# Attention with 192 queries and 1,024 keys: GpSimd issues 121 of 128 partitions of each group's store

## The chip, the cores and the metric

The kernel runs on one core of one Trainium2 chip. The core has five engines that run side by side and meet only at semaphores: TensorE (matrix products, PE in the profile), VectorE (DVE), ScalarE (ACT), GpSimd (POOL) and SyncE (SP, which here only issues transfers). Data moves between the main memory (HBM) and the on-chip memory (SBUF) on 16 DMA engines, which all queues share. A transfer is issued by an instruction on SyncE, ScalarE or GpSimd, and each of these has a queue of its own. TensorE writes its products to a second on-chip memory, PSUM.

The metric is the time of one execution on the device in microseconds (us), as the median of several runs.

## The reference

The reference is softmax attention over 16 x 32 = 512 heads. Each has 192 queries, 1,024 keys and 1,024 values of 128 numbers, all bfloat16:

```python
B, H, Sq, Sk, D = 16, 32, 192, 1024, 128
scale = q.shape[-1] ** -0.5
scores = jnp.einsum("bhqd,bhkd->bhqk", q, k) * scale
p = softmax(scores, axis=-1)
return jnp.einsum("bhqk,bhkd->bhqd", p, v)
```

Keys and values are 134 MB each, queries and output 25 MB each.

## The kernel before

**Groups, pairs and units.** The 512 heads are worked in 32 groups of 16 (`G=16`). A group has 8 pairs of heads (`PPG`). The 2 x 192 query rows of a pair make three units of 128 rows: unit A (128 rows of the first head), unit B (128 of the second) and unit S (64 of each). So a group has 24 units (`UPG`), and a unit is a tile of 128 query rows by 1,024 keys. Two pairs, six units in the order A0 B0 A1 B1 S0 S1, make one *period*; a group has four periods. Unit numbers in the text are those inside a group: unit 12 is A0 of the third period, unit 14 its A1, unit 18 is A0 of the fourth period, and unit 21 its B1.

**One unit.** TensorE makes the scores into PSUM (`s_ps`, "qk"). VectorE scales them into `ss` and finds the row's extreme in the same instruction (line 333). Four of six units then go to ScalarE, which takes the exponential into `x_sb` (line 374). The other two (A0 and B1, "shifted") go to GpSimd, which subtracts the extreme (line 208), and ScalarE takes the exponential later. TensorE transposes `x_sb` in 8 blocks ("tr", into `pt_ps`), ScalarE copies the result to `pt_sb` ("ev", lines 383 and 385), TensorE multiplies it with the values ("pv", into `o_ps`), and VectorE divides by the row sums into `ob` (line 358).

**Order.** The order of each engine is written out by hand in `PE_ORDER`, `DVE_ORDER` and `ACT_ORDER`; a tick in these lists means the same unit of the period before. GpSimd runs the shifts in the order of units and nothing else. Every engine runs its list in order, and a wait stops all that stands behind it on that engine. TensorE's transpose of a shifted unit waits for its shift; the transpose of B1 comes in the period after its scores.

**Buffers and transfers.** Keys (`kt`), queries (`qt`) and values (`vs`) of a group have two buffers each, as has the output `ob`. Keys and queries are transposed by the DMA itself (lines 148 and 152). The first two groups are loaded at the start. From then on:

- SyncE, for each group g, waits until TensorE has made all scores of group g (`s_qk`), since its buffer is used again. It then issues the keys and queries of group g + 2, and then waits for the output of group g and stores it. The store is cut by partitions into three transfers, 0 to 79, 80 to 123 and 124 to 127. The last group's output is stored in four pieces of 128 partitions each.
- ScalarE issues the values of the next group after the copy of unit 12 (`VALUES_AFTER`). Before that it waits until the same group's keys have landed (`sxk`, line 393).
- VectorE, before the first output of a group, waits until the store from that half of `ob`, two groups back, has landed (`sst`, line 354).

One row of the output has 128 numbers, 256 bytes. A partition holds 24 such rows of a group, which lie apart in main memory.

## Time and profile before

| What | Before |
|---|---|
| median of 3 runs | 1189.44 us (1187.03 to 1191.16) |
| the profiled execution | 1188.88 us, its span 1187.1 us |
| mean granted TensorE clock | 0.993 |
| TensorE busy | 1125.9 us (95%) |
| VectorE busy | 1087.6 us (92%) |
| ScalarE busy | 1080.6 us (91%) |
| GpSimd busy | 485.8 us (41%) |
| moved by DMA | 321.26 MB, mean 271 GB/s |
| packets | 790,348, of them 724,641 under 512 B |
| SyncE's queue (q1) | 192.95 MB |
| ScalarE's queue (q10) | 125.83 MB |

The profile was taken in one execution, so its parts are compared with 1188.88 us and not with the median. The span is the time from the first to the last instruction of the program. Busy times of the engines overlap and don't add up to the span. In the lists of the profile a name such as "ob<-o_ps" means that a tile is written from another; "L208" is a line of the kernel; "x256" is a count. SPq and ACTq are the transfer-issuing instructions of SyncE and ScalarE; their duration is that of the issue and not that of the transfer. The DMA share is the summed time of packets over 16 engines, and since packets overlap within an engine it can exceed 1.

### The profile page before, as it was taken

Reading aid. Unit: us, or ns where it says so; the run is one execution under the profiler, and the core shown is the slowest. Engines: PE = TensorE matmul, PEld = TensorE weight load, DVE = VectorE, ACT = ScalarE, POOL = GpSimd, SP = SyncE. Lnnn points to the kernel's source line nnn. Section 1 sums busy time; section 2 is a strip of 40 time slices with the busy share of each in tenths; the row PEclk is TensorE's granted clock in tenths of the full one; section 3 lists DMA queues with packets and bytes.
Section 4 is the critical chain, followed back from the end, with each engine's and each line's share of the span. In section 5 each row is a group of like instructions: output and inputs, shape, how many; then the busy total and the mean of one; then the engine's idle time right before and its main releaser. Section 6 shows DMA issues by size and latency. Waiting matters only on the chain.

```text
span 1187.1 us, 38884 instructions
## 1 busy us (share of the span) xinstructions
PE 1125.9 (95%) x18432; PEld 845.9 (71%) x15360; DVE 1087.6 (92%) x2304; ACT 1080.6 (91%) x1793; POOL 485.8 (41%) x262
## 2 busy tenths in 40 slices
PE   5699999999999999999999999999999999999998
PEld 2477776777777776777777767777777776677776
DVE  5589998999999998999999989999999999899997
ACT  4679998999999998999999988999999998899998
POOL 2234443444444434443444434344444343444442
PEclk9899999999999999999999999999999999999999
DMA  9999999999999999999999999999999999999981
GB/s 231 249 280 303 289 285 254 260 299 293 287 293 248 256 290 288 280 283 258 279 298 284 284 265 242 290 296 282 288 266 267 295 284 290 259 267 277 297 246 40
DMA packets 790348, 321.26 MB, mean 271 GB/s; under 512 B 724641, under 2 KB 724641, under 8 KB 790177
## 3 DMA queue, kind: packets, MB, share of 16 engines
q1 hardware_dynamic: 728257, 192.95, 84.0%
q10 hardware_dynamic: 61920, 125.83, 28.7%
q8 instruction: 132, 2.16, 0.7%
q14 instruction: 39, 0.32, 0.1%
HBM read 134.22 MB, written 25.17 MB: 134 GB/s over the span
## 4 chain that ended last, share of the span: by engine, by line
PE 43%; DMA 39%; ACT 11%; SPq 5%; ACTq 1%; issue 0%; DVE 0%
DMA kt<-in_k_dram 39%; PE o_ps L221 15%; PE pt_ps L221 15%; PE s_ps L221 14%; ACT x_sb L374 6%; SPq L148 4%; ACT pt_sb L385 3%; ACT pt_sb L383 2%; ACTq L138 1%; SPq L152 1%; SPq L138 0%; DMA vs<-in_v_dram 0%; DVE ob L358 0%; ACTq L393 0%; DVE rinv L356 0%
## 5 line engine op out<-in xcount | busy, mean ns | idle before, releaser
L333 DVE TENSOR_SCALAR_CACHE_REDUCE ss<-s_ps 128x1024 f32<-128x1024 f32 x768 | 919.5, 1220 | 83.2 <-PE s_ps L221 69.7
L208 POOL TENSOR_TENSOR x_sb<-ss,nb 128x1024 bf16<-128x1024 f32 x256 | 485.1, 1895 | 689.3 <-DVE ss L333 574.1
L374 ACT ACTIVATE x_sb<-ss,nb 128x1024 bf16<-128x1024 f32 x512 | 584.9, 1144 | 13.0 <-DVE ss L333 13.0
L306 PEld LDWEIGHTS <-pt_sb 128*128 128x128 bf16 (+1 forms) x8192 | 440.9, 104 | 194.9 <-issue 101.7
L221 PE MATMUL o_ps<-vs,pt_sb 128*128 128x128 bf16 (+1 forms) x8192 | 494.9, 219 | 0.4 <-DMA vs<-in_v_dram 0.3
L221 PE MATMUL s_ps<-kt,qt 128*128 128x512 bf16 (+1 forms) x2048 | 465.2, 385 | 24.2 <-DMA qt<-in_q_dram 23.7
L221 PE MATMUL pt_ps<-ident,x_sb 128*128 128x128 bf16 x6144 | 449.9, 220 | 33.4 <-ACT pt_sb L383 15.9
L280 PEld LDWEIGHTS <-x_sb 128*128 128x128 bf16 x6144 | 368.9, 98 | 101.5 <-issue 100.7
L385 ACT ACTIVATE pt_sb<-pt_ps 128x512 f32<-128x512 f32 x512 | 306.3, 598 | 84.6 <-PE pt_ps L221 51.5
L383 ACT ACTIVATE pt_sb<-pt_ps 128x1024 bf16<-128x1024 bf16 x256 | 260.3, 1017 | 3.6 <-PE pt_ps L221 3.6
L221 PE MATMUL o_ps<-ones,pt_sb 128*128 128x1 bf16 x2048 | 189.3, 165 | 0.0
L358 DVE TENSOR_TENSOR ob<-o_ps,rinv 128x384 bf16<-128x384 f32 x256 | 142.6, 557 | 8.7
L264 PEld LDWEIGHTS <-qt 128*128 128x128 bf16 (+1 forms) x1024 | 79.3, 103 | 41.6 <-DMA qt<-in_q_dram 18.7
L374 ACT ACTIVATION_READ_ACCUMULATOR x_sb<-ss,nb 128x1 f32 x512 | 100.3, 196 | 0.0
L333 DVE DVE_READ_ACCUMULATOR ss<-s_ps 128x1 f32 x768 | 63.7, 83 | 0.0
L356 DVE RECIPROCAL rinv<-o_ps 128x1 f32<-128x1 f32 x256 | 41.8, 163 | 4.3 <-PE o_ps L221 4.3
L346 DVE RECIPROCAL rinv<-rs 128x2 f32<-128x2 f32 x256 | 41.0, 160 | 1.1 <-ACT x_sb L374 1.1
L374 ACT ACT_TABLE_LOAD x1 | 1.3, 1283 | 0.8 <-PEq L418 0.8
L200 POOL TENSOR_SCALAR_AFFINE_SELECT ident<-ones 128x128 bf16<-128x128 bf16 x1 | 0.3, 294 | 0.1
L198 POOL MEMSET ones<- 128x128 bf16 x1 | 0.2, 205 | 0.3 <-POOLq L418 0.3
L418 POOL MEMSET const-float32-0.0<- 128x1 f32 x1 | 0.1, 99 | 0.3 <-issue 0.3
L418 POOL MEMSET const-bfloat16-1.0<- 128x1 bf16 x1 | 0.1, 102 | 0.0
(2 smaller groups left out, 0.2 us busy)
## 6 DMA issues: line engine op xcount, KB each, us to landing
vs<-in_v_dram ACTq DMA_DIRECT2D x30, 4096.0 KB, 16.3
out_dram<-ob SPq DMA_DIRECT2D x31, 480.0 KB
out_dram<-ob SPq DMA_DIRECT2D x31, 264.0 KB
vs<-in_v_dram SPq DMA_DIRECT2D x1, 4096.0 KB, 15.1
vs<-in_v_dram SPq DMA_DIRECT2D x1, 2048.0 KB, 10.4
vs<-in_v_dram SPq DMA_DIRECT2D x1, 1536.0 KB, 8.9
out_dram<-ob SPq DMA_DIRECT2D x31, 24.0 KB
kt<-in_k_dram SPq DMA_TRANSPOSE x34, 21.1
```

The source lines that it names most:

```text
L148: e.dma_start_transpose(kt[:, s, :, a * 128:b * 128], kf[h0 + a:h0 + b].rearrange("g (p t) d -> (g p) (t d)", t=KT_TILES),).then_inc(sems[ ...
L208: gp.tensor_tensor(x_sb[:, u % NX, :], ss[:, u % NSS, :], nb[:, u % NSS: u % NSS + 1].to_broadcast([128, SK]), ALU.subtract,).then_inc(s_x ...
L221: return pe.add_instruction(mybir.InstMatmult(name=nc.get_next_instruction_name(), engine=mybir.EngineType.PE, ins=[pe.lower_ap(x), pe.low ...
L264: pe.ldweights(w, tile_position=at)
L280: pe.ldweights(w, is_transpose=True, tile_position=(0, 0))
L306: pe.ldweights(w, tile_position=at)
L333: dve.tensor_scalar(ss[:, u % NSS, :], s_ps[u % 2][:].rearrange("p t k -> p (t k)"), -scale, None, ALU.mult, ALU.min, accum_out=nb[:, u % ...
L356: dve.reciprocal(rinv[:, pr % 2, sel], o_ps[pr % 2][:, 3, sel]).then_inc(s_ri, 1)
L358: dve.tensor_tensor(ob[:, so, pg], o_ps[pr % 2][:, 0:3, :], rinv[:, pr % 2, 0:3].unsqueeze(2).to_broadcast([128, 3, 128]), ALU.mult,).then ...
L374: act.activation(x_sb[:, u % NX, :], ss[:, u % NSS, :], ACT_FN.Exp, bias=nb[:, u % NSS: u % NSS + 1], scale=-1.0, accum_out=rs[:, pr % NRS ...
L383: act.activation(pt_sb[:, u % NPT], pt_ps[u % 2][:], ACT_FN.Exp, scale=-1.0).then_inc(s_ev, 1)
L385: act.activation(words(pt_sb[:, u % NPT]), words(pt_ps[u % 2][:]), ACT_FN.Copy).then_inc(s_ev, 1)
```

## The change

The store of each group but the last is split in two. GpSimd issues partitions 0 to 120 as one transfer, SyncE the other 7. GpSimd does this in the group after, in its list behind the shift of unit 18, once ScalarE has made the copy of unit 14 (`POOL_STORE=(18, 14)`) and VectorE all outputs of the group stored. SyncE issues its 7 partitions where it issued the three transfers. GpSimd's stores have semaphores of their own (`ssp`); VectorE waits for both before it writes to that half of `ob` again, and SyncE waits for both at the end. The stores of the last group are as before.

```diff
-  STORE_PARTS=((0, 80), (80, 124), (124, 128)), VALUES_AFTER=("ev", 12)):
+  POOL_STORE=(18, 14), POOL_PARTS=121, VALUES_AFTER=("ev", 12)):
...
+        ssp = [sem("ssp%d" % i) for i in range(NSO)]
...
         def store_cnt(g):
-            return 16 * len(STORE_PARTS) * (g // NSO + 1)
+            return 16 * (g // NSO + 1)
...
+        def store(e, g, a, b, lo, hi, sm):
+            rows = of[g * G + 2 * a:g * G + 2 * b].rearrange("h r d -> (h r) d").rearrange("(n p) d -> p n d", p=128)
+            e.dma_start(
+                rows[lo:hi],
+                ob[lo:hi, g % NSO, a:b].rearrange("p pg y d -> p (pg y) d"),
+            ).then_inc(sm[g % NSO], 16)
...
             def stores(g, a, b):
-                so = g % NSO
                 e.wait_ge(s_on, g * PPG + b)
-                rows = ...
-                for lo, hi in (((0, 128),) if g == NGR - 1 else STORE_PARTS):
-                    e.dma_start(rows[lo:hi], ob[lo:hi, so, a:b]...).then_inc(sst[so], 16)
+                store(e, g, a, b, 0 if g == NGR - 1 else POOL_PARTS, 128, sst)
...
             for so in range(min(NSO, NGR)):
-                n = len(range(so, NGR - 1, NSO)) * len(STORE_PARTS)
+                n = len(range(so, NGR - 1, NSO))
...
                 e.wait_ge(sst[so], 16 * n)
+                e.wait_ge(ssp[so], 16 * len(range(so, NGR - 1, NSO)))
...
+            unit, copy = POOL_STORE
             for u in range(NU):
                 if shifted(u):
                     shift(u)
+                g = u // UPG - 1
+                if u % UPG == unit and g >= 0:
+                    gp.wait_ge(s_ev, u - unit + copy + 1)
+                    gp.wait_ge(s_on, (g + 1) * PPG)
+                    store(gp, g, 0, PPG, 0, POOL_PARTS, ssp)
...
                 if pg == 0 and g >= NSO:
                     dve.wait_ge(sst[so], store_cnt(g - NSO))
+                    dve.wait_ge(ssp[so], store_cnt(g - NSO))
```

More of the change, by code (lines that the diff above doesn't have):

```diff
@@ L34, in _attention_kernel @@
 def _attention_kernel(nc, q, k, v, out, G=16, NS=2, NSS=5, NX=4, NPT=5,
-                      FIRST=((0, 2), (2, 8), (8, 16)), LAST=((0, 4), (4, 6), (6, 7), (7, 8)), STORE_PARTS=((0, 80), (80, 124), (124, 128)), VALUES_AFTER=("ev", 12)):
+                      FIRST=((0, 2), (2, 8), (8, 16)), LAST=((0, 4), (4, 6), (6, 7), (7, 8)), POOL_STORE=(18, 14), POOL_PARTS=121, VALUES_AFTER=("ev", 12)):
     B, H, SQ, D = q.shape
@@ L166, in stores @@
             def stores(g, a, b):
-                so = g % NSO
                 e.wait_ge(s_on, g * PPG + b)
-                rows = of[g * G + 2 * a:g * G + 2 * b].rearrange("h r d -> (h r) d").rearrange(
-                    "(n p) d -> p n d", p=128)
-                for lo, hi in (((0, 128),) if g == NGR - 1 else STORE_PARTS):
-                    e.dma_start(
-                        rows[lo:hi],
-                        ob[lo:hi, so, a:b].rearrange("p pg y d -> p (pg y) d"),
-                    ).then_inc(sst[so], 16)
+                store(e, g, a, b, 0 if g == NGR - 1 else POOL_PARTS, 128, sst)
             n = len(FIRST)
```

## The prediction

> **What bounds the kernel now.** I read the engine totals first, then SyncE's queue, ScalarE around its load of the values, the chain of waits, the DMA rates by stage, and last the gap on GpSimd that the new instruction goes into.

> ```profile
> PE 1125.9 (95%) x18432; PEld 845.9 (71%) x15360; DVE 1087.6 (92%) x2304; ACT 1080.6 (91%) x1793; POOL 485.8 (41%) x262
> ```

> Three engines are over 90% busy, so little is left between them; what is left has to be found by stage. The loop over 31 groups repeats, so one group's cycle is the unit to measure. ScalarE issues one load of values per group, and these are the first and last of them (30 issues, 29 cycles), from the instructions of line 138:

> ```profile
> L138 ACTq DMA_DIRECT2D vs<-in_v_dram x30: 374/375/432, 90.1 to 1133.5; - x30
> ```

> (1133.5 - 90.1) / 29 = 35.98 us a group. What would the engines alone take? In the chain of waits, TensorE's double transposes (x16) mark the four periods of a group. Here are two periods that nothing outside delayed, the second of them holding ScalarE's load issue:

> ```profile
> 259.27 1.00 PE pt_ps L221 x16
> ...
> 267.90 1.00 PE pt_ps L221 x16
> ...
> 276.79 1.00 PE pt_ps L221 x16
> ```

> 8.63 and 8.89 us (8.64 where it is read elsewhere): an undelayed group is 3 x 8.64 + 8.89 = 34.81 us. So 1.17 us a group, 34 us over 29 cycles, is delay. SyncE's queue and ScalarE in order of time show where it comes from (start, duration, what; brackets hold idle time before):

> ```profile
> 573.00 17.52 SPq L148 DMA_TRANSPOSE kt<-in_k_dram  x1
> 590.57 3.99 SPq L152 DMA_TRANSPOSE qt<-in_q_dram  x1
> 594.60 13.94 SPq L172 DMA_DIRECT2D out_dram<-ob  x3
> 608.58 16.74 SPq L148 DMA_TRANSPOSE kt<-in_k_dram  x1
> ```

> ```profile
> 594.13 0.38 ACTq L138 DMA_DIRECT2D vs<-in_v_dram  x1
> 594.56 0.60 ACT L385 ACTIVATE pt_sb<-pt_ps 128x512 f32<-128x512 f32 x1 [0.88 <-PE pt_ps L221]
> ```

> SyncE has no gap: keys 17.5, queries 4.0, stores 13.9, together 35.4, and the next keys follow at once. ScalarE stands still until the keys land (573.00 plus 21.06 in the chain = 594.06), then issues the values. ScalarE's waits between 60 and 1150 us name this directly, though part of it goes under TensorE's name (total, times, longest):

> ```profile
> ACT pt_sb L385 <- PE pt_ps L221: 45.5, 131, 9.1
> ACT pt_sb L385 <- DMA kt<-in_k_dram: 25.9, 12, 3.3
> ```

> The keys could start earlier. Their buffer is free when TensorE has made the last score product of the group that used it, and SyncE comes 7.2 us after that (601.35 against 608.58), because it is still issuing stores:

> ```profile
> 600.75 0.60 PE L221 MATMUL s_ps<-kt,qt 128*64 128x512 bf16 x4
> ```

> ```profile
> L172 SPq DMA_DIRECT2D out_dram<-ob x3: 677/6462/6714, 594.6 to 601.8; - x3
> ```

> Those are the three store issues of this group, in ns (shortest, median, longest). The parts have 480, 264 and 24 KB, and the small ones take as long as anything: issuing waits for room in a queue that drains slowly beside the values. The rates by stage of the next cycle (stretch, busy times, clock, DMA share, GB/s):

> ```profile
> 611.50:631.50 20.00, 20.00 (x338) 15.31 (x272) 19.58 (x44) 19.33 (x34) 8.84 (x5) 1.00 1.27 248
> 632.00:643.50 11.50, 11.40 (x187) 8.55 (x159) 11.04 (x24) 11.05 (x20) 3.94 (x4) 1.00 1.04 368
> 643.50:647.00 3.50, 3.50 (x75) 2.68 (x59) 3.46 (x7) 3.50 (x7) 1.88 (x1) 1.00 0.76 171
> ```

> Keys and queries, then values with the first stores, then a tail of stores at less than half the rate, behind which the next keys stand in the same queue. That tail is what the bound is made of.

> **The change, part by part.** The sum is made against the profiled execution, 1188.88 us for a span of 1187.1; the median shown is 1189.44.

> *Removed from SyncE:* per group two of three store issues, 31 times. Keys, queries and one 42 KB store are then 17.5 + 4.0 + one issue. That issue is between 0.3 us (the shortest of this line) and 7.9 (the longest); I take 0.7, as only 42 KB stand in that queue, and even 7.9 is covered: 17.5 + 4.0 + 7.9 = 29.4 of a 34.8 us cycle, after which SyncE waits for TensorE instead of coming late. The keys therefore start up to 7.2 us sooner, land before ScalarE asks, and its waits for them go. Full value: 29 x 1.17 = 33.9 us.

> *What is late next:* the DMA engines. A group moves 4.19 MB of keys, 0.79 of queries, 4.19 of values, 0.79 of output. Keys and queries take the 20.0 us of the first row (its average of 248 GB/s includes their stops). Values and all stores, 4.98 MB at the 368 of the second row, take 13.5. Together 33.5 us, below 34.81, if stores really run beside the values and the tail is gone. The margin is only 1.3 us and cycles vary (the one before took 23 us from 574 to 597 for keys and queries), so some waits stay. Full removal is 34.81 a group, no removal 35.98; I take 35.1, nearer to the floor because the 7.2 us of earlier start absorbs single long cycles. Gain 29 x 0.88 = 25.5 us.

> *Added on GpSimd:* 31 DMA issues of 726 KB, each with two waits before it. The wait for output is long met. The wait for ScalarE's copy of unit 14 ends about when the shift of unit 18 does (596.63 here; the copy is the one that begins at 596.18 and takes 0.59). Behind the issue stands the shift of unit 21, and for that waits a TensorE transpose:

> ```profile
> 594.73 1.90 POOL L208 TENSOR_TENSOR x_sb<-ss,nb 128x1024 bf16<-128x1024 f32 x1 [2.40 <-DVE ss L333]
> 599.62 1.89 POOL L208 TENSOR_TENSOR x_sb<-ss,nb 128x1024 bf16<-128x1024 f32 x1 [2.99 <-PE pt_ps L221]
> ```

> ```profile
> 604.85 0.61 PE L221 MATMUL pt_ps<-ident,x_sb 128*128 128x128 bf16 x8
> ```

> Free: 599.62 - 596.77 = 2.85 us of idle GpSimd, then 604.85 - 601.51 = 3.34 us until TensorE needs the shift's result: 6.2 us in all. No row has a DMA issued by GpSimd. Nearest are issues that wait for no room: 0.38 us for the 4 MB of values, 0.68 for the 480 KB store; the far end is 13.94, all a group's stores on SyncE. I take about 2 us, nearer the small rows as this queue is empty at each issue; up to 6.2 it costs nothing. If that cover is gone, each us costs 31.

> [...]

> *Queues the store is moved past:* on SyncE it no longer stands ahead of the next keys; on GpSimd's queue it starts some 3 us after the values' issue and shares the engines with them, and the keys that now start earlier do so too. That is the second thing that can be late, and the values have little room. They land 16.3 us after their issue, and TensorE first uses those of 594.13 at 612.84, 18.7 us after it:

> ```profile
> vs<-in_v_dram ACTq DMA_DIRECT2D x30, 4096.0 KB, 16.3
> ```

> ```profile
> 612.84 0.22 PE L221 MATMUL o_ps<-vs,pt_sb 128*128 128x128 bf16 x1
> ```

> 2.4 us are free. The 0.60 MB of the tail, moved ahead of the values' end, takes 0.60 / 0.368 = 1.6 us of them at worst; what the keys take besides is rival 3, and the rest of why I stay 0.3 us above the floor.

> *Added waits on VectorE and at the end:* a second wait before a group's first output, for a store issued some 20 us earlier; and one for GpSimd's stores on SyncE at the end, the last of which is issued half a group before. Each is between nothing and a semaphore step, under 0.1 us; taken as 0, covered by those 20 us. The last group's stores are unchanged.

> Sum: 1188.88 - 25.5 = 1163.4.

> **Rivals.** *1. GpSimd's issue outgrows its gap (slower).* Place: between the shifts of units 18 and 21. Above 6.2 us, TensorE stands still each group, and the gain is used up at 6.2 + 34/31 = 7.3 us. For it: 726 KB in rows of 256 B are some 2,900 pieces, and nothing of the kind is in the trace. Against: the values' issue with 2 KB pieces, 2,048 of them, took 0.38. At 8 us: 1155 + 31 x 1.8 = 1211; at 13.94: 1155 + 31 x 7.74 = 1395.

> *2. Hidden anyway (no change).* The DMA engines, not SyncE, set 35.98: the stores take the same time beside the keys as the tail takes now, and the keys land as late. For it: DMA share near or over 1 in all but the tail. Against: the tail at 171 GB/s and 0.76. Time 1189. [...]

> *3. The values land late (slower).* Place: TensorE's first output product of each group; it decides from a delay of 2.4 us on. Keys that start 7.2 us sooner meet the values half done. If they then get half of 368 GB/s from 9 us after the values' issue, they take about 9 x 0.184 = 1.7 MB ahead of the values' end, 4.5 us; with nothing for the tail that is 2.1 us late a group, with the tail's 1.6 it is 3.7. Cycle 36.9 to 38.5, so 1155 + 29 x 2.1 = 1216 to 1262. At a quarter of the rate instead: 2.2 us, late by nothing to 1.4, so 1155 to 1196. For it: today the values have the engines almost alone (368 GB/s, of 4.19 MB in 11.5 us). Against: the second and third store issues are held for 6.5 us each while values move, so a queue of 256 B pieces gets a small share beside 2 KB ones, and the keys are such a queue.

> **How the numbers follow.** Forecast 0.57, rival 1 0.21, rival 2 0.09, rival 3 0.13. Rival 2 is within 0.3% (3.6 us), about what a measurement here can tell. A small part of rival 3 (1155 to 1185) is still faster: faster 0.60, same 0.09, slower 0.31. Predicted 1163, from the likeliest. Its own range is 1153 (the floor of 1155 less the spread of 2 us below the median) to 1178 (half the delay kept would be 1172, and some more). The 8-in-10 range goes on to 1215, which takes in rival 2, most of rival 3, and rival 1 up to an issue of 8.1 us; outside stay about half of rival 1 (0.11), the worst of rival 3 (0.04) and a little below the floor.

> **What would show it.** SyncE: one short store, then a wait of several us for TensorE before each key load. Key loads start within 1 us of the last score product. ScalarE: 0.2 us instead of up to 3.3 before the copy behind the values' issue. The tail at 171 GB/s gone. Cycle near 35.1. GpSimd's issue under 6.2 us and TensorE's transpose of unit 21 not waiting for it. Wrong, if TensorE waits for GpSimd's shift once a group, for the values' landing, or if keys start early and land late all the same.

## The result, and the profile after

The changed kernel takes 1260.97 us (median of 4 runs, 1256.02 to 1269.7) against 1190.3 us of the kernel before, a ratio of 1.060 (95% interval 1.053 to 1.067). It is slower by 71 us where 1163 was predicted. The profiled execution took 1259.22 us, its span is 1257.5 us. First the totals of the page:

```profile
PE 1146.6 (91%) x18432; PEld 859.3 (68%) x15360; DVE 1091.2 (87%) x2304; ACT 1083.9 (86%) x1793; POOL 540.4 (43%) x293
```

The span grew by 70.4 us. TensorE is busy 20.7 us more, which is taken up below; the rest of it is standing still. The loads of values give the cycle (the instructions of their line: shortest/median/longest issue, first and last start):

```profile
L139 ACTq DMA_DIRECT2D vs<-in_v_dram x30: 374/374/425, 90.4 to 1203.0; - x30
```

(1203.0 - 90.4) / 29 = 38.37 us a group, where it was 35.98. Now the parts that the prediction spoke of. SyncE's queue and GpSimd in order of time:

```profile
629.30 0.70 SPq L146 DMA_DIRECT2D out_dram<-ob  x1
636.03 27.55 SPq L156 DMA_TRANSPOSE kt<-in_k_dram  x1
```

```profile
631.73 1.80 POOL L146 DMA_DIRECT2D out_dram<-ob  x1 [1.45 <-ACT pt_sb L394]
634.28 1.88 POOL L210 TENSOR_TENSOR x_sb<-ss,nb 128x1024 bf16<-128x1024 f32 x1 [0.75 <-PE pt_ps L229]
```

SyncE does what it was to do: one short store, then a gap, then the keys at the moment their buffer is free. GpSimd's issue takes 1.80 us and the shift behind it is on time. But the keys' issue now lasts 27.55 us in place of 17.5. The transfers say why that helped nobody (KB each, us from issue to landing):

```profile
vs<-in_v_dram ACTq DMA_DIRECT2D x30, 4096.0 KB, 20.7
out_dram<-ob POOLq DMA_DIRECT2D x31, 726.0 KB, 13.9
...
kt<-in_k_dram SPq DMA_TRANSPOSE x34, 30.3
```

The keys start 7 us sooner and land 9.2 us later after their issue (21.1 before), and the values land 20.7 us after theirs (16.3 before), when TensorE had wanted them at 18.7. That wait is now in TensorE's list, which had 0.3 us of it before:

```profile
PE o_ps L229 <- DMA vs<-in_v_dram: 49.9, 26, 3.7
```

The rates by stage of one cycle show the place. The columns are the stretch, the busy times of the engines, clock, DMA share and GB/s:

```profile
631.00:636.00 5.00, 4.32 (x75) 2.97 (x68) 3.77 (x8) 4.79 (x9) 3.52 (x2) 1.00 1.09 382
636.50:640.00 3.50, 3.50 (x62) 2.79 (x41) 3.43 (x7) 3.50 (x8) 1.02 (x1) 1.00 1.17 337
640.00:642.50 2.50, 2.50 (x37) 1.93 (x33) 2.46 (x7) 2.50 (x5) 0.87 (x1) 1.00 1.14 165
643.00:645.50 2.50, 2.50 (x57) 1.93 (x51) 2.43 (x8) 2.50 (x5) 1.89 (x1) 1.00 1.04 354
```

Nearly alone, the values move at 382 GB/s. From 636.5 GpSimd's store is beside them and the sum falls. At 640 the keys have joined, and for 2.5 us the three together move 165 GB/s; by the packet records the keys have under 12 of it.

One more thing changed that no part of the prediction held: TensorE's clock. The stretch behind the end of one of its waits for values:

```profile
651.00:656.00 5.00, 5.00 (x58) 3.90 (x48) 2.17 (x3) 1.66 (x3) 0.00 (x0) 0.71 1.27 290
```

The clock records of the trace have, between the start-up and the last group, 14 stretches at half clock, 54.6 us in all; the kernel before has none there. On TensorE the loss has two parts. It stands still for 110.9 us in place of 61.2, 49.7 us more, and its waits for values alone grew by 49.6. It is busy for 20.7 us more with the same instructions, which goes with the clock: 54.6 us at half clock would cost 27.3 by estimate, but waits lie in these stretches as well. That is a sum over records and not a proof of causes; the runs below are for that.

### The profile page after: what moved, and what is told of

It reads as the page before. It is cut to its first block, busy times and chain, and to the rows that moved or that the text cites. A ratio compares the mean times of both kernels' runs of the same rounds, so it can differ in the third digit from the quotient of the medians.

```text
span 1257.5 us, 38885 instructions
## 1 busy us (share of the span) xinstructions
PE 1146.6 (91%) x18432; PEld 859.3 (68%) x15360; DVE 1091.2 (87%) x2304; ACT 1083.9 (86%) x1793; POOL 540.4 (43%) x293
## 4 chain that ended last, share of the span: by engine, by line
DMA 62%; PE 30%; SPq 5%; ACT 3%; issue 0%; DVE 0%; ACTq 0%
DMA vs<-in_v_dram 33%; DMA kt<-in_k_dram 29%; PE o_ps L229 11%; PE pt_ps L229 10%; PE s_ps L229 9%; SPq L156 4%; ACT x_sb L383 2%; ACT pt_sb L394 1%; SPq L160 1%; ACT pt_sb L392 0%; SPq L139 0%; DVE ob L367 0%; ACTq L139 0%; ACTq L402 0%; DVE rinv L365 0%
## 5 line engine op out<-in xcount | busy, mean ns | idle before, releaser
L341 DVE TENSOR_SCALAR_CACHE_REDUCE ss<-s_ps 128x1024 f32<-128x1024 f32 x768 | 921.2, 1220 | 149.7 <-PE s_ps L229 132.5
L314 PEld LDWEIGHTS <-pt_sb 128*128 128x128 bf16 (+1 forms) x8192 | 449.0, 105 | 255.3 <-issue 164.4
L229 PE MATMUL o_ps<-vs,pt_sb 128*128 128x128 bf16 (+1 forms) x8192 | 503.2, 220 | 51.0 <-DMA vs<-in_v_dram 49.9
L229 PE MATMUL s_ps<-kt,qt 128*128 128x512 bf16 (+1 forms) x2048 | 472.3, 389 | 27.2 <-DMA qt<-in_q_dram 26.6
L229 PE MATMUL pt_ps<-ident,x_sb 128*128 128x128 bf16 x6144 | 456.3, 221 | 29.5 <-ACT pt_sb L394 17.6
L288 PEld LDWEIGHTS <-x_sb 128*128 128x128 bf16 x6144 | 373.6, 99 | 95.0 <-issue 94.5
L146 POOL DMA_DIRECT2D out_dram<-ob x31 | 56.1, 1810 | 29.0 <-ACT pt_sb L394 28.7
## 6 DMA issues: line engine op xcount, KB each, us to landing
vs<-in_v_dram ACTq DMA_DIRECT2D x30, 4096.0 KB, 20.7
out_dram<-ob POOLq DMA_DIRECT2D x31, 726.0 KB, 13.9
vs<-in_v_dram SPq DMA_DIRECT2D x1, 4096.0 KB, 15.4
kt<-in_k_dram SPq DMA_TRANSPOSE x34, 30.3
```

Of the source, the lines that this page charges most:

```text
L146: e.dma_start(rows[lo:hi], ob[lo:hi, g % NSO, a:b].rearrange("p pg y d -> p (pg y) d"),).then_inc(sm[g % NSO], 16)
L229: return pe.add_instruction(mybir.InstMatmult(name=nc.get_next_instruction_name(), engine=mybir.EngineType.PE, ins=[pe.lower_ap(x), pe.low ...
L288: pe.ldweights(w, is_transpose=True, tile_position=(0, 0))
L314: pe.ldweights(w, tile_position=at)
L341: dve.tensor_scalar(ss[:, u % NSS, :], s_ps[u % 2][:].rearrange("p t k -> p (t k)"), -scale, None, ALU.mult, ALU.min, accum_out=nb[:, u % ...
```

## The experiments

### Is it the early keys or the store?

Theory A says that the keys, starting while values are in flight, hold everything up whoever stores. Theory B says that GpSimd's store takes the engines from the values. Four kernels were made to tell them apart.

*No store by GpSimd* (it leaves out the store of partitions 0 to 120 of groups 0 to 30; the waits for it go too):

```diff
-                    store(gp, g, 0, PPG, 0, POOL_PARTS, ssp)
+                    pass
```

> Part left out: GpSimd's store, so partitions 0 to 120 of the output of groups 0 to 30 are never stored; keys start as early as in the changed kernel. Theory A (the keys' transposes that start while values are in flight hold everything up, whoever stores): values still land later than the 16.3 us of before, 17 to 20, keys in over 25 us, TensorE still waits for values, 1180 to 1230 us. Theory B (the store in GpSimd's queue takes the engines from the values): values land in 14 to 15 us, keys in about 21, cycle at its floor of 34.8 us, 1153 to 1162 us.

Measured: 1148.61 us, ratio 0.969 (0.967 to 0.971). Its loads of values, and TensorE's wait for them:

```profile
L139 ACTq DMA_DIRECT2D vs<-in_v_dram x30: 374/374/425, 89.9 to 1092.7; - x30
```

```profile
PE o_ps L228 <- DMA vs<-in_v_dram: 0.9, 1, 0.9
```

The cycle is (1092.7 - 89.9) / 29 = 34.58 us, the floor. The keys start just as early as in the changed kernel, take 25.9 us to land, and nobody waits. Theory A falls: early keys alone cost nothing. Two of Theory B's numbers were off too: it had the keys in after about 21 us, and the values after 14 to 15, where they took 15.8. The 35.98 us of before were the price of the stores; whether by their place in SyncE's queue or by their bytes this run can't say, for it takes away both.

*Keys five units and three units later,* the store by GpSimd as in the change:

```diff
-                    e.wait_ge(s_qk, last_u + 1)
+                    e.wait_ge(s_qk, last_u + 1 + 5)
```

> One number changed: SyncE issues the keys of group g+2 five units (about 7.2 us) after the last score product of group g, which is where the kernel before issued them; GpSimd's store unchanged. Theory A: keys land in 20 to 22 us and values in 15.5 to 17.5, TensorE's wait for values goes from 49.9 us to under 10, 1160 to 1190 us. Theory B: values still land in 19 to 21 us, 1230 us or more.

> As the run with five units, but three units late (about 4.3 us). Theory A: between the changed kernel and the run with five units, keys in 22 to 27 us, 1165 to 1220 us. Theory B: no difference from the changed kernel, 1250 to 1270 us.

Measured: 1243.18 us with five (ratio 1.051, 1.047 to 1.054), 1267.28 us with three (1.070, 1.064 to 1.076). With five the values still land after 19.5 us, though the keys start 7 us later. So the store delays them without early keys, as Theory B had it (1230 us or more with five, 1250 to 1270 with three). TensorE's wait for values does fall, from 49.9 to 23.2 us with five, but ScalarE's for keys rises from 19.0 to 42.7.

*The store a period earlier,* meant to run beside keys and queries and to be done before the values:

```diff
-POOL_STORE=(18, 14)
+POOL_STORE=(12, 8)
```

> GpSimd's store moved a period and more ahead (behind the shift of unit 12 and the copy of unit 8), so that it runs beside the keys and queries and is done before the values start; keys start as early as in the changed kernel. Theory A: keys and values still meet, and the store now meets the keys too: 1220 to 1290 us. Theory B: values land in 14 to 16 us and keys in 22 to 24 us, 1160 to 1185 us.

Measured: 1352.63 us, but its runs spread from 1312 to 1400 us at a lower clock than all others (0.918 to 0.947), so no ratio is given. Both theories were below it. The edit did not do what it was meant to: in the packet records (of the longest run) part of the store still moves behind the first packet of the values in 18 of 30 groups, a third of its bytes in all. So this run decides nothing between the theories, and what a store wholly beside the transposes costs is not shown.

### What does the store cost by itself?

Theory C says that a store in GpSimd's queue costs the DMA engines more time than one in SyncE's, Theory D that it costs the same and only its meeting with the keys hurts. Two kernels keep the keys back until values and stores have landed, one with GpSimd's store (its edit is shown) and one with SyncE's three parts:

```diff
                     e.wait_ge(s_qk, last_u + 1)
+                    e.wait_ge(svl[(g - 1) % NS], load_cnt(g - 1))
+                    if g >= 3:
+                        e.wait_ge(ssp[(g - 3) % NSO], store_cnt(g - 3))
+                        e.wait_ge(sst[(g - 3) % NSO], store_cnt(g - 3))
```

> The changed kernel, but SyncE issues a group's keys only after the values and both parts of the store in flight have landed, so values and store have the engines to themselves and the stage can be measured alone. The cycle gets longer by the latency of each hand-over, 37 to 39.5 us, 1220 to 1300 us. Theory C (a store in GpSimd's queue costs the DMA engines more time than one in SyncE's, even with nothing else moving): from the values' issue to the last landing it takes at least 1 us longer than in the run with SyncE's stores. Theory D (the store costs the same by itself; what costs is that keys meet it): the two stages agree within 1 us or GpSimd's is shorter.

> The kernel before, with the same wait before the keys (values and store landed). Its stage from the values' issue to the last landing should be 17.5 to 19 us by the tail seen before; cycle 36.5 to 39 us, 1200 to 1280 us. Theory C: at least 1 us a group faster than the run with GpSimd's store. Theory D: equal or slower.

Measured: 1300.93 us with GpSimd's store (ratio 1.097, 1.094 to 1.101) and 1247.43 us with SyncE's (1.051, 1.046 to 1.056). The stage can be read from the issue of the values to the next issue of keys, which waits for nothing else. GpSimd's:

```profile
650.81 0.37 ACTq L139 DMA_DIRECT2D vs<-in_v_dram  x1
```

```profile
669.18 17.78 SPq L156 DMA_TRANSPOSE kt<-in_k_dram  x1
```

and SyncE's:

```profile
660.11 0.37 ACTq L138 DMA_DIRECT2D vs<-in_v_dram  x1
```

```profile
677.07 18.17 SPq L148 DMA_TRANSPOSE kt<-in_k_dram  x1
```

18.4 us here against 17.0; over all groups the medians are 19.7 and 17.8. So values and store take 1.9 us longer when GpSimd issues the store, with no keys beside them, and the values land after 19.6 us in place of 16.2. Theory C's number came out and D's did not. But it is not engine time that grew, as Theory C has it: the packets of one of GpSimd's stores took 45 us in all, and 2,904 packets of 256 bytes at 18 ns, their median in the kernel before, would take 52 by estimate. Nor is the queue the only difference. GpSimd's first packet comes 8.5 us after the values' issue, SyncE's issue begins 0.5 us after it (medians), and the parts have 121 and 7 partitions in place of 80, 44 and 4. (Of the 53 us between the two kernels about half goes with the clock again, 0.960 against 0.982: TensorE is busy for 24.1 us more.)

*Half of the partitions in GpSimd's queue* (`POOL_PARTS=64`), and *the store in ScalarE's queue,* 112 partitions issued behind the values:

> The changed kernel with partitions 0 to 63 in GpSimd's queue and 64 to 127 in SyncE's. Theory C: the loss goes with the bytes in GpSimd's queue, about half of 71 us, 1210 to 1235 us. Theory D: the loss goes with how early the keys start; SyncE's larger store sits ahead of the keys again, 1185 to 1205 us.

> Partitions 0 to 111 go through ScalarE's hardware queue, issued behind the values (after the copy of unit 14), 112 to 127 through SyncE's; keys start as early as in the changed kernel, GpSimd issues nothing. The issue costs ScalarE 0.4 us a group if there is room in its queue (12 us in all), several us if not. Theory C: values land in 16 to 17.5 us, keys in under 27, 1160 to 1195 us (later only by what ScalarE stands still at the issue). Theory D: keys meet values and store as in the changed kernel, 1225 to 1270 us.

Measured: 1197.61 us with 64 partitions, ratio 1.009 (1.006 to 1.012). That is below Theory C's range and inside Theory D's, but without D's reason: the keys start 7.2 us after the values' issue at the median, as in the changed kernel. Values land after 17.7 us. So the loss is not in proportion to the bytes in GpSimd's queue. With ScalarE's queue it is 1238.2 us (1.043, 1.039 to 1.047), again inside Theory D's range, but for another reason. Its issues of the store, and ScalarE behind one:

```profile
L146 ACTq DMA_DIRECT2D out_dram<-ob x31: 328/3445/6768, 91.2 to 1220.8; - x31
```

```profile
656.31 3.63 ACTq L146 DMA_DIRECT2D out_dram<-ob  x1
659.99 1.15 ACT L383 ACTIVATE x_sb<-ss,nb 128x1024 bf16<-128x1024 f32 x1 [2.27 <-DVE ss L341]
```

The issue behind the values takes 3.4 us at the median, against 0.33 at the shortest, and ScalarE's next exponential begins when it ends. The DMA side went as Theory C had it, or better: values land after 15.2 us, keys after 25.4, and TensorE waits 0.3 us for values. So a store of nearly the same size, with keys issued as soon as in the change, did not delay the values when ScalarE's queue carried it behind them. It had 112 partitions and not 121, so this run does not tell the queue from the cut.

### Why does GpSimd's store cost more?

64 partitions had cost 11 us and 121 cost 71. The packet records give a reason. Each store of 121 partitions is 176 packets of 4096 bytes and 11 of 2048: eleven equal shares of 67,584 bytes, which is 11 partitions of 6,144. 121 is 11 x 11. Beside them stand 80 packets of 64 bytes and 5 of 32, sixteen and one for each of five, as if five engines had a share without data. If those shares are engines, eleven engines carry 67.6 KB beside their full part of the values, five carry none, and the eleven set when the values land. That is Theory E. 112 partitions would make sixteen shares of 7, and 110 again eleven, of 10. Only `POOL_PARTS` differs in these kernels:

> The changed kernel with partitions 0 to 111 in GpSimd's queue and 112 to 127 in SyncE's. Theory E (the trace shows the store of 121 partitions as eleven equal shares of 11 partitions, so eleven engines carry it beside their full share of the values and those set when the values land): 112 partitions fall into sixteen shares of 7, 43 KB an engine in place of 67.6. By the line through no store (0 KB, values in after 15.3 us), 64 partitions (24.6 KB, 17.2) and 121 (67.6 KB, 20.2) the values are in after 18.4 us, TensorE's wait for them falls from 50 us to under 10, 1185 to 1215 us. Theory C (the bytes in GpSimd's queue cost, however they are shared): 93% of the bytes, values in after 19.8 us, 1245 to 1258 us.

> As the run with 112, but 110 partitions, which have no divisor from 12 to 16: eleven shares of 10 partitions, 61.4 KB an engine. Theory E: values in after 19.7 us, 1235 to 1255 us, far from the run with 112 though the bytes differ by 2%. Theory C: within 10 us of the run with 112.

> 96 partitions in GpSimd's queue (sixteen shares of 6, 36.9 KB an engine), 32 in SyncE's. Theory E: values in after 18.0 us, 1180 to 1205 us. Theory C: three quarters of the loss, 1230 to 1245 us.

Measured: 112 partitions 1207.84 us (ratio 1.020, 1.015 to 1.024), 110 partitions 1256.8 us (1.061, 1.056 to 1.065), 96 partitions 1208.74 us (1.021, 1.017 to 1.025). Two partitions fewer cost 49 us. The issue and landings of 112:

```profile
L146 POOL DMA_DIRECT2D out_dram<-ob x31: 1293/1293/1451, 93.0 to 1194.4; - x31
```

```profile
vs<-in_v_dram ACTq DMA_DIRECT2D x30, 4096.0 KB, 19.6
out_dram<-ob POOLq DMA_DIRECT2D x31, 672.0 KB, 9.8
```

```profile
PE o_ps L229 <- DMA vs<-in_v_dram: 20.8, 21, 2.2
```

and of 110:

```profile
L146 POOL DMA_DIRECT2D out_dram<-ob x31: 1688/1688/1838, 93.5 to 1242.4; - x31
```

```profile
vs<-in_v_dram ACTq DMA_DIRECT2D x30, 4096.0 KB, 21.1
out_dram<-ob POOLq DMA_DIRECT2D x31, 660.0 KB, 13.7
```

```profile
PE o_ps L229 <- DMA vs<-in_v_dram: 54.4, 25, 5.9
```

The smaller store lands 3.9 us later. Between these two the number of shares decides, not the bytes, and Theory C falls; SyncE's part differs a little as well (16 and 18 partitions), a seventh of the store. Theory E's numbers came out only in part. 112 partitions are inside its range, 110 are 2 us above it and 96 are 4 us above it; the values landed later with 112 than its line said (19.1 us to the last packet, 18.4 expected), and TensorE's wait was 20.8 us, not under 10. Of the 48 us between the two spans (1258.2 and 1210.2) TensorE stands still for 22.8 and is busy for the other 25.2, and the longer waits go with a lower clock: 61.4 us at half clock with 110 partitions, none with 112. No run separates the wait from the clock that follows it.

That the shares are engines shows in how the values go on once the store is nearly done. Here they are almost alone, first with 121 partitions (the run that holds the keys back), then with 112 (the run with late keys, below); the last three columns are clock, DMA share and GB/s:

```profile
665.50:667.00 1.50, 1.50 (x38) 1.03 (x32) 1.47 (x4) 1.50 (x3) 1.50 (x1) 1.00 0.73 273
```

```profile
575.50:577.00 1.50, 1.50 (x22) 1.15 (x20) 1.50 (x3) 1.26 (x3) 0.00 (x0) 1.00 1.06 406
```

Over all groups the values move at 274 GB/s from 14 to 16 us after their issue in the first run, and at 396 from 12 to 14 us in the second. The ratio is 0.69, and 11/16 is 0.69. That fits five engines that have finished their part and eleven that are behind by what the store took.

*112 partitions, and the keys four units later:*

> 112 partitions in GpSimd's queue, and the keys issued four units (5.8 us) after the last score product, so that values and store are nearly done. Theory E with a share for the keys' early start: 1175 to 1200 us, less than the run with 112 alone. If the early start costs nothing once the shares are even, it is slower than the run with 112, 1195 to 1220 us.

Measured: 1194.93 us, ratio 1.007 (1.005 to 1.009). Here the early keys do cost something, 13 us, although without a store they cost nothing: values land after 17.6 us and TensorE's wait for them is 1.1 us. That agrees with the 165 GB/s of the changed kernel, which are seen where all three streams meet; why they lose so much there is not shown.

### Eleven engines in SyncE's queue, and a small share for GpSimd

Does the uneven split hurt by itself, or only in GpSimd's queue? Two kernels are the one before with other cuts, `((0, 121), (121, 128))` and `((0, 112), (112, 128))`, all in SyncE's queue. A third gives GpSimd 48 partitions.

> The kernel before, with its store cut into partitions 0 to 120 and 121 to 127, both in SyncE's queue. Theory F (eleven shares cost only where each turn is as long as the values' or longer, as in GpSimd's queue): the store trickles beside the values as before, values in after 16 to 16.5 us, 1180 to 1200 us, within 10 us of the run with 112. Theory G (any store on eleven engines delays the values by its bytes there): values in after 18 us or more, 1210 us or more, at least 25 us above the run with 112.

> The kernel before, with its store cut into partitions 0 to 111 and 112 to 127, both in SyncE's queue and both on sixteen engines. One issue less than before, so the keys come a little sooner; the tail behind the values stays. Both theories: 1175 to 1195 us.

> The changed kernel with 48 partitions in GpSimd's queue (sixteen shares of 3, 18.4 KB an engine) and 80 in SyncE's. By the runs with 64 (1198) and 96 (1209), if the loss goes on falling with the share: 1185 to 1195 us, no better than before. If SyncE's 80 partitions now finish beside the values and the tail goes: 1165 to 1180 us, better than before.

Measured: 1213.62 us with 121 (ratio 1.020, 1.017 to 1.023) and 1203.2 us with 112 (1.013, 1.009 to 1.017). The values land after 15.8 and 16.4 us. So in SyncE's queue the split costs 10.4 us, and in GpSimd's the like of it (110 against 112) costs 49. By the landing of the values Theory F holds, since the split does not touch them. By the time it does not: 1213.62 us is above its range, inside Theory G's, and a little over 10 us above the run with 112, though far from G's 25. Both kernels were expected faster; the three parts of the kernel before are better than either cut. The share of 48 partitions takes 1201.38 us (1.010, 1.007 to 1.014): the loss does not go on falling below 64, and no kernel with a complete output was faster than the one before.

## Why the prediction was wrong

**SyncE's queue: right.** Two store issues less, one of 0.70 us, a gap, and keys on time. The run without GpSimd's store shows the floor that was worked out as 34.81 us a group: 34.58, and 1148.61 us against the 1155 of full removal, with 726 KB a group less to move.

**GpSimd's issue: right.** About 2 us were taken, 1.80 measured, inside the 6.2 us of cover; TensorE waits for no shift. Rival 1 did not occur: the 2,904 rows cost 1.80 us.

**The DMA engines, under "What is late next" and "Queues the store is moved past": wrong, and this is the step that failed.** Two terms were mis-sized. One is "Values and all stores, 4.98 MB at the 368 of the second row, take 13.5". That rate was read where a store trickles beside the values, and was used as if every byte of the store would move at it on all engines alike. In GpSimd's queue it does not: its packets have 4096 bytes, 178 ns each at the median, against the values' 2048 in 84, and with 121 partitions they fall into eleven shares, eleven engines of sixteen by the 0.69 above. With the keys out of the way values and store took 19.7 us from the values' issue, and some 2 us of that pass before the values' first packet (1.9 at the median in the changed kernel). The other is "1.6 us of them at worst" for what the store can take of the values' 2.4 us. One share of 16.5 packets is, by estimate, 16.5 x 0.178 = 2.9 us on its engine, and the values landed 3.4 us later with the keys out of the way (19.6 against 16.2), 4.4 us later with them. With sixteen shares and late keys it is 1.3 us, and TensorE hardly waits.

**Keys that land before ScalarE asks: wrong as a consequence.** They were issued 7 us sooner, but by the packet records their queue moved under 20 GB/s from 8 to 16 us after the values' issue and 251 from 23 to 24 us, when the values were in (means over the groups); 30.3 us to landing used up the lead, and ScalarE's waits for keys only fell from 25.9 to 19.0 us. Rival 2 had this step, but its time, 1189, did not come out.

**Rival 3: right in its place, wrong in its culprit.** The values did land late at TensorE's first output product, and 1216 to 1262 us were worked out for it. That 1261 falls into this range is partly luck, for in 20.7 of the 70.4 us TensorE is busy longer at a lower clock (0.974 against 0.993), which the rival did not have. It blamed the keys for most of the delay (4.5 of 6.1 us), and without the store the keys delay nothing; it was the store. What spoke against it, that a queue of 256-byte pieces gets a small share beside 2 KB ones, was said of the keys and was right for them (under 12 of 165 GB/s where all three met). It was never asked of the store in its new queue, whose packets are 4 KB.

**Left out altogether:** the number of engines that 121 partitions reach, and the clock. The first was open to see in the kernel before. Its three stores of a group, of 80, 44 and 4 partitions, have 31 packets of 4 bytes in SyncE's queue, as many as 16 + 11 + 4 engines would leave with one each. With 121 and 7 partitions that queue has 403 packets fewer (727,854 against 728,257), 13 for each of the 31 groups, and 18 is 11 + 7; with 112 and 16 it has 31 more (728,288), one a group, and 32 is 16 + 16.

## What to carry to other kernels

Before a transfer is moved to another queue, work out for both queues how many engines it reaches and how long its packets are beside those it will share them with; the 368 GB/s read here beside a trickle did not hold for the same bytes in another queue. For a transfer that runs beside one with a deadline, ask what shares its partitions make: in GpSimd's queue 110 in eleven shares against 112 in sixteen was 49 us here. And for every load in the way, read the time from landing to first use. Here it was 2.4 us, and a delay beyond it cost more than itself: with 110 partitions TensorE stood still for 22.8 us more than with 112, and it was busy for 25.2 us longer.

## What was not expected of the hardware

*GpSimd's issue time went with the partitions of one share, not with the bytes.* The issues of 48, 64 and 96 partitions, from three runs:

```profile
L146 POOL DMA_DIRECT2D out_dram<-ob x31: 833/833/993, 94.6 to 1183.8; - x31
```

```profile
L146 POOL DMA_DIRECT2D out_dram<-ob x31: 971/973/1133, 93.1 to 1180.6; - x31
```

```profile
L146 POOL DMA_DIRECT2D out_dram<-ob x31: 1178/1178/1336, 93.2 to 1191.6; - x31
```

With 112, 110 and 121 partitions it is 1293, 1688 and 1803 ns. In shares of 3, 4, 6, 7, 10 and 11 partitions these lie within 25 ns of one line, (1803 - 833) / 8 = 121 ns for each partition of a share, and it is this that shows the eleven shares without the packets.

*Queues that met shared by the length of their packets.* In the kernel before, SyncE's store, in packets of 256 bytes, moves 43 GB/s from 9 to 13 us after the values' issue, beside 343 of the values in packets of 2048: 1 to 8, as the packets. With 112 partitions in GpSimd's queue, in packets of 4096 bytes, it is 241 beside 120 from 9 to 10 us, 2 to 1. (Both are means over the groups.) In both the share of a queue went with the length of its packets.

*Key transposes stopped close behind packets of the instruction queue.* In the run without GpSimd's store the packet records fall below 20 GB/s for 3.3 us a group, mostly in single stops of about 1 to 1.5 us that begin within 1 us of a 16 KB packet of the instruction queue. In the kernel before, 34 of the 35 pauses of more than 0.4 us between packets of a key load begin within 1 us behind such a packet. No run tried it, so it is a coincidence in time that is seen, not a cause.

Open is what exactly costs the 10 us that remain with 112 partitions and late keys against the kernel before, and what a store wholly beside the transposes would cost.
